# Five weight buffers and an earlier end of the weight splits, in a kernel of top-k attention and a gated FFN

## The chip, the cores and the metric

The kernel runs on one NeuronCore of a Trainium2 chip. The metric is device time in microseconds (us), lower is better. The engines are named as in the profile: PE (TensorE; PEld is its loading of weights), DVE (VectorE), ACT (ScalarE), POOL (GpSimd) and SP (SyncE, which here issues nearly all DMAs). Each engine works through its own list of instructions in order.

## The reference

Attention over 8 batches, 8 heads, 576 tokens and a head size of 64, in which every query keeps its 32 largest scores; then a gated feed-forward network (FFN) over all 4608 tokens. Everything is float32.

```python
scores = scale * np.matmul(q, k.transpose(0, 1, 3, 2))            # (8, 8, 576, 576)
kth = np.partition(scores, -top_k, axis=-1)[..., -top_k:-top_k + 1]
scores = np.where(scores >= kth, scores, -1000000000.0)
attn = np.exp(scores - np.max(scores, axis=-1, keepdims=True))
attn = attn / (np.sum(attn, axis=-1, keepdims=True) + 1e-09)
attn_out = np.matmul(attn, v)
x = attn_out.transpose(0, 2, 1, 3).reshape(4608, 512)
gate = 1.0 / (1.0 + np.exp(-(x @ w_gate)))                        # (4608, 1536)
return (gate * (x @ w_val)) @ w_out                               # (4608, 512)
```

## The kernel before

**Attention** goes in steps (loop variable `n`): a step is one block of 128 queries of a pair of heads in a batch. A step is named by batch, block and pair, as in e_0_3_2 (batch 0, block 3, pair 2). For a step PE makes the scores (pss; L269 and its neighbours in batch 0, L239 later), ACT copies them (s), DVE finds the 24 largest of 72-column segments (L338 to L344), ACT and POOL find what lies under them (L350, L356), DVE the threshold (L366), ACT the exponentials (L287), DVE the product with the mask (e, L292). PE transposes e (pt, L378), ACT copies that (et, L379), and PE multiplies by the values (po, L414), which gives the FFN's input xh and xl, an upper part and a rest.

**The FFN** works on units of tokens: units 0 to 2 have 256, the others 384. Its float32 products are made of three matmuls on upper parts and rests, so each weight tile is split too. There are 18 weight tiles of 1 MB: 0 to 11 hold gate and value weights (four to a group, three groups), 12 to 17 the output weights (two to a group). For a unit, `wide` does one tile of the first kind: 24 matmuls into pz (L475 to L477), the gate on ACT, DVE and ACT (gf, gh), the rest gl on POOL. `narrow` does half a tile of the second kind: 12 matmuls into po2 (L496 to L498; the profile writes po), added to acc.

**Splitting a weight tile** (`split_weights`) takes: a load of the raw tile (wraw, L135, a pool of two), ACT's L152 and L151, DVE's L153 (wt_lead, a pool of one), L161 and L162 (wt_frac, a pool of one), ACT's L163 (upper part), PE's L168, L169 and L170 (the rest, in PSUM), ACT's L171 (the rounded rest), and a store to DRAM (ws, L172). The result lies in a buffer of the pool "w". Tiles 4 to 11 and 14 to 17 are used from there by unit 0 (`fresh`; the profile writes w_split); all later uses load the tile again from DRAM into a buffer of the same pool (L461, tile w). The tiles are split in the order 0 to 3, 12, 13, 4 to 7, 14, 15, 8 to 11, 16, 17.

**What sets the order.** The loop over steps writes out attention, the splits that are due, and FFN tasks. `HELD`, 20, is the number of half splits (two to a tile) due by step `SOON`; the last 16, eight tiles, are spread evenly over the steps from there to `RUSH`:

```python
due = HELD * (n + 1) // SOON
if n >= SOON:
    due = HELD if not todo else HELD + (2 * n_w - HELD) * (n - SOON) // (RUSH - SOON)
```

`todo` is empty until unit 0's input is written out at the end of step 9, so these 16 half splits fall to the steps 10 and on. Unit 0's FFN tasks are written out between the splits, each as soon as its tile is split. When the last split is done the pools of the split are given back, and the pools that take their room open: among them one more score tile ("spare"), with which scores are made three steps ahead instead of two. What the loop writes out is then put into each engine's order by a scheduler that weighs priorities and readiness, at build time. A tile that needs a buffer waits until the last use of the tile five (or four) before it in its pool.

Of the kernel before, what the change touches and what calls it, by code (L numbers as in the profile page):

```python
# [30 lines left out]
def tile_topk_attention_then_gated_ffn(  # L31
# [19 lines left out]
    FG = NE = NP  # L51
# [15 lines left out]
    FETCH, ASK, AHEAD = 2, 4, 2  # L67

    orders = ([*range(1, NG), 0], [*range(NG)])
    SOON, RUSH = 8, 15  # L70
    RAISE = 200
    HELD = 2 * (2 * FG + NE // 2)
    MILES = [(512, 256), (832, 512), (1152, 768), (1536, 1152), (1984, 1536), (2624, 2112)]
# [35 lines left out]
    pools, fresh, copies, ahead, requests = {"first": bkr}, {}, [], [], []  # L109

    def ffn_pools():
        for name, bufs in (("w", 4), ("f2", 3), ("f4", NE), ("fg", FG + 1)):
            pools[name] = ctx.enter_context(tc.tile_pool(name=name, bufs=bufs))

    def split_weights():
# [401 lines left out]
    def run(general):  # L517
# [27 lines left out]
        if not general:  # L545
            ffn_pools()
            splits = split_weights()
# [176 lines left out]
```

## Time and profile before

| | us |
|---|---|
| median of 3 runs | 1564.49 |
| lowest and highest of them | 1562.36, 1564.89 |
| the profiled execution | 1562.55 |
| its span, from first to last instruction | 1560.7 |

Of the span PE is busy 97%, DVE 82%, ACT 72%, POOL 68%. A busy time is the union of an engine's instructions, so what is missing from the span is idle time. Matmuls overlap: the length of one is longer than the distance to the next (0.28 us against 0.12 for 256 columns).

### The profile page before, as it was taken

How to read it: one execution, taken by the hardware profiler on the slowest of the kernel's cores; microseconds unless marked ns; L12 is line 12 of the kernel's file. 1: busy time of each engine (PE TensorE's matmuls, PEld its weight loads, DVE VectorE, ACT ScalarE, POOL GpSimd, SP SyncE). 2: the span in 40 equal slices, each digit the busy share in tenths (PEclk: the TensorE clock that was granted, in tenths of full speed). 3: DMA queues.
4: the chain of work that ended last, by engine and by line, in shares of the span. 5: the costliest groups of instructions: out<-in, count | busy, mean ns of one | idle time of the engine just before them, and what ended most of it. 6: DMA issues, size and time to landing. Idle time of an engine off the chain costs nothing.

```text
span 1560.7 us, 33841 instructions
## 1 busy us (share of the span) xinstructions
PE 1510.3 (97%) x10586; PEld 1378.4 (88%) x10586; DVE 1284.5 (82%) x5806; ACT 1116.0 (72%) x2405; POOL 1063.5 (68%) x1756
## 2 busy tenths in 40 slices
PE   6779999999999999999999999999999999999998
PEld 2346689999999999899999999999999999999998
DVE  7999868999988789888988879988898888888311
ACT  8998968787877687776776766777777777677221
POOL 4666658898766786787666876787766886676211
PEclk8999999999999999999999999999999999999999
DMA  7763598887655755566555665565564675465574
GB/s 251 258 222 134 214 359 314 290 282 291 230 187 200 245 197 206 182 229 221 204 178 198 223 239 189 195 238 196 208 223 168 208 250 194 173 223 177 193 273 158
DMA packets 88894, 344.14 MB, mean 220 GB/s; under 512 B 9856, under 2 KB 36992, under 8 KB 57984
## 3 DMA queue, kind: packets, MB, share of 16 engines
q1 hardware_dynamic: 88560, 341.58, 62.5%
q8 instruction: 86, 1.41, 0.4%
q14 instruction: 104, 0.85, 0.2%
q10 hardware_dynamic: 144, 0.29, 0.1%
HBM read 313.52 MB, written 28.31 MB: 219 GB/s over the span
## 4 chain that ended last, share of the span: by engine, by line
PE 74%; DVE 9%; POOL 6%; ACT 6%; issue 2%; DMA 2%; SPq 0%; POOLq 0%; ACTq 0%
PE pz L476 11%; PE pz L477 11%; PE pz L475 11%; PE pss L239 8%; PE po L414 6%; PE pt L378 6%; PE po L496 5%; PE po L498 5%; PE po L497 5%; POOL u L356 3%; DVE cand L338 2%; DVE e L292 2%; PE po L428 2%; ACT e L287 2%; ACT under L350 1%
## 5 line engine op out<-in xcount | busy, mean ns | idle before, releaser
L356 POOL TENSOR_TENSOR u<-s,under 128x288 f32<-128x288 f32 x576 | 456.0, 814 | 138.1 <-ACT under L350 127.4
L338 DVE MAX8 cand<-s 128x8 f32<-128x72 f32 x2304 | 346.6, 217 | 64.6 <-ACT s L246 56.3
L475 PE MATMUL pz<-xh,w 128*128 128x384 f32 (+1 forms) x1184 | 390.4, 332 | 1.1 <-DVE acc L502 0.7
L477 PE MATMUL pz<-xh,w 128*128 128x384 f32 (+1 forms) x1184 | 391.1, 331 | 0.0
L476 PE MATMUL pz<-xl,w 128*128 128x384 f32 (+1 forms) x1184 | 390.1, 330 | 0.3 <-POOL xl L448 0.3
L292 DVE SCALAR_TENSOR_TENSOR e<-s,kths,e 128x576 f32<-128x576 f32 x288 | 280.7, 977 | 0.9 <-ACT e L287 0.7
L350 ACT ACTIVATE under<-s,leads 128x576 bf16<-128x576 f32 x288 | 222.6, 774 | 80.4 <-DVE leads L342 33.1
L366 DVE MAX8 kths<-u 128x8 f32<-128x584 f32 x288 | 219.1, 761 | 45.0 <-POOL u L357 43.3
L287 ACT ACTIVATE e<-s,st 128x576 f32<-128x576 f32 x288 | 209.6, 771 | 62.9 <-POOL st L346 62.4
L483 POOL TENSOR_TENSOR gl<-gf,gh 128x384 fp32r<-128x384 f32 (+1 forms) x156 | 151.6, 972 | 116.5 <-ACT gh L482 112.7
L475 PEld LDWEIGHTS pz<-xh,w 128*128 128x128 f32 x1184 | 222.8, 189 | 2.4 <-DVE acc L502 1.0
L476 PEld LDWEIGHTS pz<-xl,w 128*128 128x128 f32 x1184 | 223.3, 189 | 0.8 <-POOL xl L448 0.6
L477 PEld LDWEIGHTS pz<-xh,w 128*128 128x128 f32 x1184 | 223.1, 189 | 0.3
L379 ACT ACTIVATE et<-pt 128x384 f32<-128x384 f32 x384 | 177.9, 486 | 27.9 <-PE pt L378 26.0
L496 PE MATMUL po<-gh,w 128*128 128x384 f32 (+1 forms) x592 | 194.6, 334 | 0.7 <-DVE acc L502 0.6
L497 PE MATMUL po<-gl,w 128*128 128x384 f32 (+1 forms) x592 | 194.9, 330 | 0.0
L498 PE MATMUL po<-gh,w 128*128 128x384 f32 (+1 forms) x592 | 194.3, 330 | 0.0
L246 ACT ACTIVATE s<-pss 128x576 f32<-128x576 f32 x252 | 161.2, 640 | 41.3 <-PE pss L239 40.5
L378 PE MATMUL pt<-ident,e 128*128 128x128 f32 x1152 | 179.6, 274 | 7.9 <-ACT et L379 4.2
L239 PE MATMUL pss<-k,qh 128*128 128x288 f32 (+2 forms) x588 | 164.9, 298 | 1.5 <-ACT s L246 1.5
L378 PEld LDWEIGHTS pt<-ident,e 128*128 128x128 f32 x1152 | 140.9, 141 | 24.6 <-ACT et L379 6.4
L239 PE MATMUL pss<-k,ql 128*128 128x288 f32 (+2 forms) x588 | 159.9, 294 | 0.0
(108 smaller groups left out, 2897.3 us busy)
## 6 DMA issues: line engine op xcount, KB each, us to landing
w<-ws SPq DMA_DIRECT2D x222, 1024.0 KB, 5.0
v<-in_v_dram SPq DMA_DIRECT2D x68, 352.0 KB, 3.2
wraw<-in_w_dram SPq DMA_DIRECT2D x36, 512.0 KB, 4.9
ws<-w_split SPq DMA_DIRECT2D x18, 1024.0 KB, 4.6
qraw<-in_q_dram SPq DMA_DIRECT2D x140, 128.0 KB, 3.1
kraw<-in_k_dram SPq DMA_DIRECT2D x56, 288.0 KB, 4.0
out_dram<-acc SPq DMA_DIRECT2D x40, 192.0 KB, 4.8
out_dram<-acc SPq DMA_DIRECT2D x12, 128.0 KB, 5.3
```

Source lines behind the costliest of these rows:

```text
L239: nc.tensor.matmul(ps[:, half, o : o + n], x[:, h * P : (h + 1) * P], ks[h][:, k0 : k0 + n], start=t == 0, stop=t == len(todo) - 1,)
L287: nc.scalar.activation(e[:, j], s[:, j], AF.Exp, bias=st[:, j : j + 1], scale=1.0 / SHRINK)
L292: nc.vector.scalar_tensor_tensor(e[:, j], s[:, j], kth[j], e[:, j], op0=ALU.is_ge, op1=ALU.mult, accum_out=st[:, 4 + j : 5 + j])
L338: nc.vector.max(cand[:, j, 8 * g : 8 * g + 8], s[:, j, g * SEG : (g + 1) * SEG])
L356: nc.gpsimd.tensor_tensor(u[:, j, part], s[:, j, part], under[:, j, part], op=ALU.mult)
L378: nc.tensor.transpose(pt[:, c], ef[:, k0 : k0 + P], ident)
L475: nc.tensor.matmul(ps, wt[:, u, 0, d], xh, start=d == 0, stop=False)
L476: nc.tensor.matmul(ps, wt[:, u, 0, d], xl, start=False, stop=False)
L477: nc.tensor.matmul(ps, wt[:, u, 1, d], xh, start=False, stop=d == NP - 1)
L496: nc.tensor.matmul(ps, wt[:, e % 2, 0, f], gh, start=f == 0, stop=False)
L497: nc.tensor.matmul(ps, wt[:, e % 2, 0, f], gl, start=False, stop=False)
L498: nc.tensor.matmul(ps, wt[:, e % 2, 1, f], gh, start=False, stop=f == FG - 1)
```

## The change

Two numbers: the pool "w" has five buffers of 1 MB instead of four, and `RUSH` is 12 instead of 15. So the due number of half splits is 28, 32 and 36 (all) at steps 10, 11 and 12; before it was 24, 26, 29, 31, 33 and 36 at steps 10 to 15.

```diff
-    SOON, RUSH = 8, 15
+    SOON, RUSH = 8, 12
...
-        for name, bufs in (("w", 4), ("f2", 3), ("f4", NE), ("fg", FG + 1)):
+        for name, bufs in (("w", 5), ("f2", 3), ("f4", NE), ("fg", FG + 1)):
```

As built, all engines' orders differ from step (0, 2, 0) on. Three places follow.

DVE, before, from the split of tile 11 to that of tile 16 (names: kths, e are attention's of the steps (0, 4, 1) and on; gf_0_2_2 is unit 0, group 2, tile 10):

```order
L153 SCALAR_TENSOR_TENSOR wt_lead_11_1984<-wt_lead_11_1984,minus_zero_168 128x1024
L342 MAX leads_122<-cand_0_4_3_2861 128x8
L366 MAX kths_121<-u_0_4_1_2683 128x8
L161 TENSOR_SCALAR wraw_11_1981<-wt_lead_11_1984 128x1024
L292 SCALAR_TENSOR_TENSOR e_0_4_1_2682,st_0_4_1_2680<-s_0_4_1_2163,kths_121,e_0_4_1_2682 128x576
L162 SCALAR_TENSOR_TENSOR wt_frac_11_1985<-wraw_11_1981 128x1024
L366 MAX kths_121<-u_0_4_2_2770 128x8
L296 RECIPROCAL st_0_4_1_2680<-st_0_4_1_2680 128x1
L481 SCALAR_TENSOR_TENSOR gf_0_2_2_1975<-gf_0_2_2_1975,pz_0_2_2_1_1962 128x256
L366 MAX kths_121<-u_0_4_3_2866 128x8
L153 SCALAR_TENSOR_TENSOR wt_lead_16_2135<-wt_lead_16_2135,minus_zero_168 128x1024
L161 TENSOR_SCALAR wraw_16_2132<-wt_lead_16_2135 128x1024
```

DVE, the changed kernel, from the split of tile 11 to wt_frac of tile 17:

```order
L153 SCALAR_TENSOR_TENSOR wt_lead_11_1808<-wt_lead_11_1808,minus_zero_168 128x1024
L161 TENSOR_SCALAR wraw_11_1805<-wt_lead_11_1808 128x1024
L481 SCALAR_TENSOR_TENSOR gf_0_2_2_1799<-gf_0_2_2_1799,pz_0_2_2_1_1786 128x256
L162 SCALAR_TENSOR_TENSOR wt_frac_11_1809<-wraw_11_1805 128x1024
L153 SCALAR_TENSOR_TENSOR wt_lead_16_1960<-wt_lead_16_1960,minus_zero_168 128x1024
L161 TENSOR_SCALAR wraw_16_1957<-wt_lead_16_1960 128x1024
L162 SCALAR_TENSOR_TENSOR wt_frac_16_1961<-wraw_16_1957 128x1024
L481 SCALAR_TENSOR_TENSOR gf_0_2_3_1951<-gf_0_2_3_1951,pz_0_2_3_1_1938 128x256
L153 SCALAR_TENSOR_TENSOR wt_lead_17_2011<-wt_lead_17_2011,minus_zero_168 128x1024
L161 TENSOR_SCALAR wraw_17_2008<-wt_lead_17_2011 128x1024
L502 SCALAR_TENSOR_TENSOR acc_0_1_0_1473<-po2_0_2_0_1979,acc_0_1_0_1473 128x256
L162 SCALAR_TENSOR_TENSOR wt_frac_17_2012<-wraw_17_2008 128x1024
```

Attention's instructions, which stood between the splits, are gone from there: the four splits follow each other with only unit 0's FFN between.

ACT, before, from the split of tile 10 to that of tile 11 (under and et are attention):

```order
L151 ACTIVATE wt_lead_11_1984<-wraw_11_1981 128x1024
L171 ACTIVATE w_split_10_1844<-wrest_10_0_1936 128x512
L171 ACTIVATE w_split_10_1844<-wrest_10_1_1941 128x512
L379 ACTIVATE et_0_2_3_2629<-pt_0_3_3_0_2710 128x3x128
L379 ACTIVATE et_0_2_3_2629<-pt_0_3_3_1_2715 128x3x128
L350 ACTIVATE under_0_4_2_2771,sums_0_4_2_2768<-s_0_4_2_2579,leads_122 128x576
L163 ACTIVATE w_split_11_1980<-wt_lead_11_1984 128x2x512
L152 ACTIVATE minus_zero_168<-wraw_16_2132 128x1024
L480 ACTIVATE gf_0_2_2_1975<-pz_0_2_2_0_1949 128x256
L350 ACTIVATE under_0_4_3_2867,sums_0_4_3_2864<-s_0_4_3_2587,leads_122 128x576
L379 ACTIVATE et_0_2_3_2629<-pt_0_3_3_2_2720 128x3x128
L384 ACTIVATE et_0_4_0_2797<-pt_0_4_0_0_2798 128x4x128
```

ACT, the changed kernel, from the split of tile 10 to that of tile 16:

```order
L171 ACTIVATE w_split_10_1748<-wrest_10_1_1765 128x512
L480 ACTIVATE gf_0_2_2_1799<-pz_0_2_2_0_1773 128x256
L163 ACTIVATE w_split_11_1804<-wt_lead_11_1808 128x2x512
L152 ACTIVATE minus_zero_168<-wraw_16_1957 128x1024
L482 ACTIVATE gh_0_2_2_1771<-gf_0_2_2_1799 128x256
L151 ACTIVATE wt_lead_16_1960<-wraw_16_1957 128x1024
L171 ACTIVATE w_split_11_1804<-wrest_11_0_1816 128x512
L171 ACTIVATE w_split_11_1804<-wrest_11_1_1821 128x512
L163 ACTIVATE w_split_16_1956<-wt_lead_16_1960 128x2x512
L480 ACTIVATE gf_0_2_3_1951<-pz_0_2_3_0_1925 128x256
L152 ACTIVATE minus_zero_168<-wraw_17_2008 128x1024
L482 ACTIVATE gh_0_2_3_1923<-gf_0_2_3_1951 128x256
```

Here too attention is gone from between. L151 of tile 16 stands ahead of both L171 of tile 11, as it stood ahead of the second of them before.

SP, which issues the DMAs, before, from the store of tile 10 on (w_0_0 to w_0_3 are unit 0's loads of tiles 0 to 3):

```order
L172 DMA ws10_133<-w_split_10_1844 128x2048
L135 DMA wraw_17_2262<-in_w_dram 128x1024 x2
L172 DMA ws11_134<-w_split_11_1980 128x2048
L172 DMA ws16_139<-w_split_16_2131 128x2048
L461 DMA w_0_0_2312<-ws0_123 128x2048
L461 DMA w_0_1_2347<-ws1_124 128x2048
L461 DMA w_0_2_2382<-ws2_125 128x2048
L192 DMA kraw_5_0_0_5444<-in_k_dram 128x576
L192 DMA kraw_5_0_1_5450<-in_k_dram 128x576
L172 DMA ws17_140<-w_split_17_2261 128x2048
L211 DMA qraw_1_0_1_2659<-in_q_dram 128x256
```

SP, the changed kernel, from the store of tile 10 on:

```order
L172 DMA ws10_133<-w_split_10_1748 128x2048
L135 DMA wraw_17_2008<-in_w_dram 128x1024 x2
L172 DMA ws11_134<-w_split_11_1804 128x2048
L172 DMA ws16_139<-w_split_16_1956 128x2048
L461 DMA w_0_0_2058<-ws0_123 128x2048
L461 DMA w_0_1_2093<-ws1_124 128x2048
L461 DMA w_0_2_2128<-ws2_125 128x2048
L461 DMA w_0_3_2163<-ws3_126 128x2048
L192 DMA kraw_5_0_0_5444<-in_k_dram 128x576
L192 DMA kraw_5_0_1_5450<-in_k_dram 128x576
L172 DMA ws17_140<-w_split_17_2007 128x2048
L211 DMA qraw_1_0_1_2659<-in_q_dram 128x256
```

Four loads of w, not three, now stand ahead of the keys (kraw), of the store of tile 17 and of two loads of queries; the load of values ahead of the store of tile 10 is gone from there.

## Rows read from the trace of the kernel before

**Rows 1.** Page, busy us (share of the span) and instructions of two engines.
```profile
PE 1510.3 (97%) x10586; PEld 1378.4 (88%) x10586; DVE 1284.5 (82%) x5806; ACT 1116.0 (72%) x2405; POOL 1063.5 (68%) x1756
```

**Rows 2.** Busy time of each engine by stretch (columns in the first row).
```profile
core 0: us, PE busy (x) PEld busy (x) DVE busy (x) ACT busy (x) POOL busy (x), PEclk, DMA share, GB/s
...
98.00:112.00 14.00, 11.08 (x56) 7.97 (x58) 14.00 (x55) 12.32 (x22) 8.43 (x12) 0.88 0.71 273
112.00:143.00 31.00, 29.55 (x193) 21.07 (x188) 31.00 (x144) 25.88 (x56) 22.84 (x37) 1.00 0.30 100
143.00:176.00 33.00, 30.74 (x200) 21.18 (x199) 30.68 (x120) 31.43 (x61) 19.86 (x30) 1.00 0.60 207
176.00:207.00 31.00, 27.80 (x175) 21.75 (x171) 23.20 (x62) 23.26 (x42) 14.15 (x25) 1.00 0.66 241
207.00:278.00 71.00, 69.52 (x607) 63.69 (x607) 56.76 (x292) 53.39 (x129) 55.21 (x93) 1.00 0.92 347
278.00:1556.00 1278.00, 1273.22 (x9086) 1209.46 (x9084) 1040.38 (x4780) 881.63 (x1953) 888.26 (x1478) 1.00 0.62 214
```

**Rows 3.** PE's waits from 176 to 207: total us, times, longest us.
```profile
PE pz L477 <- ACT w_split L171: 1.6, 1, 1.6
PE po L498 <- ACT w_split L171: 0.8, 2, 0.6
PE wrest L170 <- DVE wt_frac L162: 0.8, 1, 0.8
```

**Rows 4.** PE's waits from 143 to 176, the same columns.
```profile
PE pt L378 <- ACT et L379: 1.4, 2, 0.7
PE pss L269 <- ACT s L270: 0.7, 1, 0.7
```

**Rows 5.** PE's waits over the whole span, first and last of 17 rows.
```profile
PE pss L269 <- ACT s L270: 11.6, 8, 3.7
...
PE po L424 <- DVE rs L440: 0.2, 1, 0.2
```

**Rows 6.** PE in order of time, 180 to 198: start us, us, instruction, idle before.
```profile
180.47 0.62 PE L170 MATMUL wrest<-wt_frac,plus 128*128 128x512 f32 x2
...
183.61 0.39 PE L477 MATMUL pz<-xh,w_split 128*128 128x256 f32 x1 [1.62 <-ACT w_split L171]
...
194.31 1.88 PE L168 MATMUL wrest<-wt_lead,ident 128*128 128x512 f32 x4
...
197.96 0.38 PE L498 MATMUL po<-gh,w_split 128*128 128x256 f32 x1 [0.60 <-ACT w_split L171]
```

**Rows 7.** ACT in order of time, 181 to 198.
```profile
181.96 1.11 ACT L151 ACTIVATE wt_lead<-wraw 128x1024 f32<-128x1024 f32 x1
182.97 1.07 ACT L171 ACTIVATE w_split<-wrest 128x512 fp32r<-128x512 f32 x2
...
194.44 1.37 ACT L152 ACTIVATE minus_zero<-wraw 128x1024 f16<-128x1024 f32 x1
...
196.29 1.14 ACT L151 ACTIVATE wt_lead<-wraw 128x1024 f32<-128x1024 f32 x1 [0.22 <-PE wrest L168]
197.33 1.06 ACT L171 ACTIVATE w_split<-wrest 128x512 fp32r<-128x512 f32 x2
```

**Rows 8.** Page, the mask products: count, busy us, mean ns, idle before.
```profile
L292 DVE SCALAR_TENSOR_TENSOR e<-s,kths,e 128x576 f32<-128x576 f32 x288 | 280.7, 977 | 0.9 <-ACT e L287 0.7
```

**Rows 9.** Tile wraw, 140 to 210: from issue to landing.
```profile
DMA to landing us min/median/max: 3.8/4.6/6.6
```

**Rows 10.** Page, DMA issues: loads of w, count, KB each, median us to landing.
```profile
w<-ws SPq DMA_DIRECT2D x222, 1024.0 KB, 5.0
```

**Rows 11.** Tile w, 190 to 240: from issue to landing.
```profile
DMA to landing us min/median/max: 6.0/8.9/11.0
```

**Rows 12.** SP's waits over the span, first row: total us, times, longest us.
```profile
SPq L461 <- PE pz L477: 282.6, 97, 7.2
```

**Rows 13.** SP in order of time, 189 us.
```profile
189.09 0.81 SPq L135 DMA_DIRECT2D wraw<-in_w_dram x2
```

## Prediction

> **What bounds the kernel now.** I read the busy times first. TensorE (PE) is busy 1510.3 us of the span, VectorE (DVE) 1284.5 [rows 1]: PE is the engine whose idle time can be won. Then I read the same table stage by stage, to see where PE idles [rows 2]. From 278 us to the end it idles 1278.00 - 1273.22 = 4.8 us in 1278. The idle time sits at the start: 2.9 us in 98 to 112, 1.5 in 112 to 143, 2.3 in 143 to 176, 3.2 in 176 to 207, 1.5 in 207 to 278. Until 143 us DVE has no idle time at all (31.00 of 31), so DVE sets the pace there; from 143 to 176 DVE (30.68 of 33) and ScalarE (ACT, 31.43 of 33) set it together. After that PE sets it.
>
> The list of what PE waited for says which waits these are. In 176 to 207 all three are for weight splits, 1.6 + 0.8 + 0.8 us: ACT's rounding of the rest (L171) and DVE's wt_frac [rows 3]. In 143 to 176 they are attention's: 1.4 for et, 0.7 for scores [rows 4]. In the list for the whole span, 17 rows that begin and end as shown, there is no row in which PE waits for a load of w [rows 5].
>
> **The change, part by part.**
>
> *The fifth buffer.* SP waits 282.6 us for PE to be done with a weight tile [rows 12]: a load goes out as soon as a buffer is free, so with four buffers each load has three tiles of PE's work to land in. 222 loads in some 1350 us are one tile in 6.1 us, so 18 us; landing takes 5.0 in the median [rows 10], and 6.0 to 11.0 in the busiest stretch, 190 to 240 [rows 11]. The fourth tile of cover isn't needed; after the splits I cost the buffer at nothing. If that cover were gone, PE would show waits for w, each worth what the landing exceeds the cover. Around 200 us four loads instead of three now stand ahead of the keys and the store of tile 17 in SP's order. The last of them waits for tile 16, as the third did before, so nothing behind it waits for a later event; one more MB goes ahead of the keys, which are first needed some 25 us on.
>
> *The earlier splits.* As built, the order parts from the old one at about 113 us, for the splits only from tile 15 on (143 us). Counted with durations of the trace, an estimate: DVE work ahead of wt_frac of tiles 15, 8 and 9 grows by 2 to 3 us, ahead of tile 10's it falls by 2.7, ahead of tiles 11, 16 and 17 by 8 to 10. What moved behind the splits is attention: between wt_frac of tiles 9 and 17, six mask multiplications (L292) of 0.98 us are gone [rows 8], 5.9 us, with maxima and smaller ones. It is not lost: DVE idles 7.8 us in 176 to 207 and 14.2 in 207 to 278 [rows 2], and can do it there. So DVE's and ACT's total work stays; what counts is which PE waits go.
>
> Tile 10: PE's last L170 was done at 180.47 + 0.62 = 181.09, but the matmuls went on only at 183.61, after a wait of 1.62 [rows 6], because L171 began only at 182.97, behind attention's operations and L151 of tile 11 on ACT [rows 7]. Now no attention stands between. In its place the first L170 must wait for wt_frac: by the same counting DVE is done with it at about 175.5 and PE asks for it at about 175.2, which is too near to call. I price this as the shorter waits of this kind, 0.6 us. Gain 1.0.
>
> Tiles 11, 16, 17: PE then runs through four splits and their 24 matmuls with nothing else to do, so each tile's own chain shows: L168 ends, ACT does L151 of the *next* tile, then L171, then PE's third matmul. Before the change this chain already ran so for tile 16: L168 from 194.31, L151 at 196.29 released by it, L171 at 197.33, PE back at 197.96 after 0.60 us [rows 6, 7]. I take 0.60 for 11 and 16 and 0.2 for 17, which has no next tile; together 1.4 against 0.8 + 0.8 now [rows 3]. Gain 0.2. Bounds: nothing (if PE's own L169 and L170 cover it) and 1.62 each, the longest wait of this kind, which would be +3.3 over the three.
>
> Raw tiles: the pool holds two, so the load of tile 16 waits for wt_frac of tile 10, that of 17 for 11. Before, that load of tile 17 went out at 189.09 [rows 13] and the first operation on it (L152) started at 194.44 [rows 7], 5.35 us later; one transfer takes 3.8 to 6.6 [rows 9]. In the new order ACT comes to tile 16 about 5.7 us after that event (L170, L168 and 24 matmuls on PE, then L480 and L163 on ACT). I put 0.3 us for both tiles; bounds 0 and 2 x 1.0.
>
> The waits of 143 to 176: two stand between the same neighbours as before; the third (0.7, for et) has new neighbours. Gain 0.4, bounds 0 and 0.7. In 207 to 278 idle is 1.5 us [rows 2]; the loads of unit 0's last group go out some 8 us earlier, and the first scores of batch 1 stand 8 us of PE work later. I take half, 0.7; bounds 0 and 1.5, and a loss as large.
>
> Sum: 1.0 + 0.2 + 0.4 + 0.7 - 0.3 = 2.0 us gained. The profiled execution took 1562.55 us (span 1560.7 and 1.85 around it), so it would take 1560.5; the median of the three runs shown is 1.9 above it, 1564.49, and the same step from there gives 1562.5.
>
> Two rules of the Trainium skill speak to this. What the row shows: where splits stood among attention, PE lost 1.62 us to L171 queued behind attention [rows 6, 7]; where they stood alone, 0.60. "Perfetto Trace Analysis", Optimization Strategy, says that stages with different limits may gain from being interleaved; the change does the opposite with the last four tiles. By the rule these would cost more, which is the third rival below; by the rows 0.6 a tile. The second: granted clock is 0.88 of full in 98 to 112, where PE idles 2.9 of 14 us, and 1.00 in 176 to 207, where it idles 3.2 of 31 [rows 2]. "TensorE: Matmul & The Clock Gate", on oscillation, says that idle stretches throttle the engine again. With waits of 0.6 us between 5 us of work I expect 1.00; one fall like that in 98 to 112 would cost 0.12 x 14 = 1.7 us.
>
> **The rivals.** *More is won.* If the earlier splits free PE from all that it waits for between 143 and 278 us, it gains 2.3 + 3.2 + 1.5 = 7.0: 1557.5. For it: DVE has 8 to 10 us less to do before the last splits. Against: the chain within a tile remains, and by the same counting PE's own work until the last of them falls by 4 to 5 us, so PE can't be there much earlier either.
>
> *Nothing changes.* The splits of 15, 8 and 9 come later by 2 to 3 us of DVE work, PE waits there, and what tiles 10 to 17 win is only given back: 1564.5. For it: until 176 us DVE has hardly any idle time to take the delay up [rows 2]. Against: the list of PE's waits for 143 to 176 has no row of a split [rows 4], so these tiles were early enough.
>
> *Slower: the last four tiles become one serial chain* (what the rule on interleaving would come to here). The place is L152 on the raw tiles 16 and 17. Cover is about 5.7 us; weight loads in 190 to 240 needed up to 11.0 [rows 11]. At that landing time each of the two tiles costs 5 us with nothing else on PE's list: 9 to 10 us less the gain, 1572. It decides from about 8.2 us landing on (2 x 2.5 us more than cover pays for the 2.0 gained and 3.1 beyond). Against: in 176 to 207 the DMA engines are busy 0.66 [rows 2], and raw transfers landed within 6.6.
>
> Besides, everything behind 207 us is in a new order, and its 4.8 us of idle after 278 are drawn anew: 3 us either way.
>
> **How the numbers follow.** 0.2% is 3.1 us, about what a measurement of this kernel tells from no change. Chances: the forecast 0.50 (-0.5 to -4, mostly inside 0.2%), more is won 0.22, nothing 0.14, the serial chain or a bad draw later 0.14. Faster: 0.22 and some 0.11 of the forecast, 0.33; slower 0.15 (the chain and a little of "nothing" with a bad draw); the same 0.52. Predicted: 1562.5. The range goes from the whole gain, 1557.5, to 1567.5, which takes in a chain that is half covered and the later draw; the full chain is left out.
>
> **What would show it.** Right: in 143 to 207 PE's idle falls from 5.5 to about 4; L171 waits of about 0.6 for tiles 11 and 16, one wait for wt_frac at tile 10; no row of PE for w; DVE idle in 180 to 200 and busy in 200 to 222; granted clock 1.00 from 112 us on. Wrong: idle of ACT before L152 for raw tiles, waits of PE for w around 205 to 220, a clock under 1.00 there, or a sum of idle after 278 that differs by more than 3 us.

## The result, and the profile after

The changed kernel takes 1575.38 us in the median of six runs (1574.82 to 1575.67), the kernel before 1564.69 beside it (six runs, 1562.36 to 1566.32): a ratio of 1.0069, 95% interval 1.0056 to 1.0082. It is slower by 10.7 us, well outside the range. The profiled execution took 1575.31 us, its span 1573.5 against 1560.7.

Busy time by stretch in the changed kernel, the columns of [rows 2]:

```profile
core 0: us, PE busy (x) PEld busy (x) DVE busy (x) ACT busy (x) POOL busy (x), PEclk, DMA share, GB/s
98.00:112.00 14.00, 10.00 (x48) 7.03 (x48) 12.48 (x51) 11.90 (x23) 6.51 (x10) 0.88 0.74 265
112.00:143.00 31.00, 29.06 (x201) 21.29 (x200) 30.89 (x146) 26.13 (x55) 25.23 (x38) 1.00 0.32 112
143.00:176.00 33.00, 31.87 (x206) 22.66 (x206) 32.86 (x120) 31.53 (x60) 16.30 (x23) 1.00 0.56 205
176.00:207.00 31.00, 28.50 (x179) 22.50 (x178) 19.38 (x52) 20.68 (x34) 8.72 (x19) 1.00 0.83 311
207.00:278.00 71.00, 69.50 (x618) 65.58 (x617) 59.95 (x285) 54.35 (x136) 57.41 (x102) 1.00 0.92 349
278.00:1556.00 1278.00, 1264.78 (x9001) 1198.73 (x9000) 1035.67 (x4792) 880.00 (x1956) 893.85 (x1482) 1.00 0.61 212
```

In 143 to 207 us, where the splits were moved, PE's idle time fell from 5.5 to 1.13 + 2.50 = 3.6 us. What was won there is small beside what came after it: from 278 us on PE idles 13.2 us in 1278 instead of 4.8.

What PE waited for from 176 to 207, to be read beside [rows 3]:

```profile
PE pz L477 <- ACT w_split L171: 1.1, 1, 1.1
PE po L498 <- ACT w_split L171: 1.0, 2, 0.8
PE wrest L170 <- DVE wt_frac L162: 0.4, 1, 0.4
```

And three rows of ACT's timeline, where it comes to the raw tiles of the last splits:

```profile
182.19 1.39 ACT L152 ACTIVATE minus_zero<-wraw 128x1024 f16<-128x1024 f32 x1 [0.54 <-DMA wraw<-in_w_dram]
188.41 1.36 ACT L152 ACTIVATE minus_zero<-wraw 128x1024 f16<-128x1024 f32 x1 [0.95 <-DMA wraw<-in_w_dram]
...
190.26 1.13 ACT L151 ACTIVATE wt_lead<-wraw 128x1024 f32<-128x1024 f32 x1 [0.23 <-PE wrest L168]
```

The serial chain that the prediction named as the slower rival shows in its beginnings: ACT waits 0.54 and 0.95 us for raw tiles. Only the first can reach PE, within the wait of 1.1 us for L171 above; behind the second, L151 waited for PE anyway (0.23 us, for L168). In the list of PE's waits over the whole span, now 20 rows, none is for a load of w.

**A ledger of lost time.** Windows cut the two kernels at different places of the work, so most numbers below are from a ledger: for each pair of neighbouring matmuls of a trace the time from start to start, less the usual one for that line and shape in the kernel before (its median; for the lines of attention whose median holds waits, the mean of the lowest 85%), summed up to a given time, less the same sum of the kernel before. It counts waits, half clock and mere wider spacing alike. At the end it must give the difference of the spans, and does: 12.7 against 12.8 us. One caution: the profiled execution of the kernel before took 1562.55 us, some 2 us less than the medians of its other runs, so totals stand about 2 us too high against the medians (the first experiment's own profiled execution was 3 us below its median, too); the steps between columns are what to read. A pair that lies across an edge goes whole to one side: at 98 us, and in the third and fourth experiments at 540, that moves a column by up to 1.5 us. In stretches where a kernel has the same order as the kernel before, the steps in these columns stay within 0.6 us.

| kernel | at 98 us | 278 | 310 | 420 | 540 | end | 98 to 278 | 310 to 420 | 540 to end |
|---|---|---|---|---|---|---|---|---|---|
| changed | +0.5 | -2.7 | -2.0 | +3.2 | +3.7 | +12.7 | -3.2 | +5.2 | +9.0 |

So three steps: the split stage wins 3.2 us, 310 to 420 us loses 5.2, and the long rest loses 9.0 in small waits.

### The profile page after: what moved, and what is told of

The parts are those of the page before. It is cut to its first block, busy times and chain, and to the rows that moved or that the text cites. A ratio compares the mean times of both kernels' runs of the same rounds, so it can differ in the third digit from the quotient of the medians.

```text
span 1573.5 us, 33811 instructions
## 1 busy us (share of the span) xinstructions
PE 1517.4 (96%) x10586; PEld 1384.8 (88%) x10586; DVE 1281.7 (81%) x5806; ACT 1112.8 (71%) x2405; POOL 1064.8 (68%) x1756
## 4 chain that ended last, share of the span: by engine, by line
PE 38%; DVE 6%; POOL 4%; ACT 3%; issue 1%; DMA 0%; POOLq 0%; ACTq 0%
PE pz L476 6%; PE pz L477 6%; PE pz L475 6%; PE pss L239 4%; PE po L496 3%; PE po L497 3%; PE po L498 3%; PE pt L378 3%; PE po L414 3%; POOL u L356 2%; DVE cand L338 2%; DVE kths L366 1%; DVE e L292 1%; ACT e L287 1%; PE po L428 1%
## 5 line engine op out<-in xcount | busy, mean ns | idle before, releaser
L356 POOL TENSOR_TENSOR u<-s,under 128x288 f32<-128x288 f32 x576 | 461.0, 822 | 125.8 <-ACT under L350 116.6
L338 DVE MAX8 cand<-s 128x8 f32<-128x72 f32 x2304 | 347.9, 218 | 81.9 <-ACT s L246 73.1
L292 DVE SCALAR_TENSOR_TENSOR e<-s,kths,e 128x576 f32<-128x576 f32 x288 | 279.2, 972 | 0.3
L378 PE MATMUL pt<-ident,e 128*128 128x128 f32 x1152 | 182.5, 277 | 8.8 <-DVE e L292 5.3
L246 ACT ACTIVATE s<-pss 128x576 f32<-128x576 f32 x252 | 161.3, 640 | 39.5 <-PE pss L239 39.1
L378 PEld LDWEIGHTS pt<-ident,e 128*128 128x128 f32 x1152 | 141.7, 142 | 26.7 <-DVE e L292 7.7
```

The source lines that it names most:

```text
L292: nc.vector.scalar_tensor_tensor(e[:, j], s[:, j], kth[j], e[:, j], op0=ALU.is_ge, op1=ALU.mult, accum_out=st[:, 4 + j : 5 + j])
L338: nc.vector.max(cand[:, j, 8 * g : 8 * g + 8], s[:, j, g * SEG : (g + 1) * SEG])
L356: nc.gpsimd.tensor_tensor(u[:, j, part], s[:, j, part], under[:, j, part], op=ALU.mult)
L378: nc.tensor.transpose(pt[:, c], ef[:, k0 : k0 + P], ident)
```

## The experiments

Theories at the start: **redraw** (the change alters the order which the scheduler draws for everything behind it, and that order, not a part of the change, carries the loss), **fifth buffer** and **earlier look-ahead** (each costs time by itself; look-ahead, because the "spare" pool opens three steps earlier). All differences are against the kernel before unless said otherwise. Beside the runs I compared the rows that TensorE executes in each kernel's built order, without the running numbers of tiles; "parts" and "joins" below are places in these lists, in us of the kernel before.

**1. The fifth buffer alone.** Kernel before with

```diff
-        for name, bufs in (("w", 4), ("f2", 3), ("f4", NE), ("fg", FG + 1)):
+        for name, bufs in (("w", 5), ("f2", 3), ("f4", NE), ("fg", FG + 1)):
```

> The weight pool has five buffers; the split stays beside seven steps, so nothing but the fifth buffer is changed. Theory 'fifth buffer' (loads of w tiles come one tile earlier, and the order behind the split stage is worse with them, whatever the split does): 1572 us or more, with some 10 us of idle TensorE after 278 us. Theory 'look-ahead' (the pools that the split stage leaves behind open three steps earlier, and with them scores, queries and keys are asked one step further ahead from the twelfth step on): 1563 to 1566 us, idle after 278 us about 5 us as before. Theory 'redraw' (each change of the order draws the small late waits anew, and no single part carries the loss): between 1562 and 1578 us, with late waits at other places than in the changed kernel.

1585.92 us, ratio 1.0129 (1.0113 to 1.0146): worse than both parts together.

**2. The earlier split alone.** Kernel before with

```diff
-    SOON, RUSH = 8, 15
+    SOON, RUSH = 8, 12
```

> Four weight buffers as before; the last eight tiles are split beside four steps. Theory 'fifth buffer': 1562 to 1565 us, the idle time of 143 to 207 us falls by some 2 us, idle after 278 us about 5 us. Theory 'look-ahead': 1572 us or more, with 10 us or more idle after 278 us. Theory 'redraw': between 1560 and 1578 us, with late waits at other places than in the changed kernel.

1575.78 us, ratio 1.0074 (1.0060 to 1.0088).

**3. The look-ahead begun where it was.** Changed kernel with

```diff
-                    next(splits, None)
-                    splits = None
+                    opening, splits = splits, None
...
+            if n == 15 and not general:
+                next(opening, None)
```

> The changed kernel (five buffers, split beside four steps), but the pools that follow the split stage open at the sixteenth step, as in the kernel before, and so the look-ahead of one more step begins there too. Theory 'look-ahead': 1562 to 1566 us, idle after 278 us about 5 us. Theory 'fifth buffer': 1572 us or more, as the changed kernel. Theory 'redraw': between 1560 and 1578 us, its late waits not those of the changed kernel.

1579.80 us, ratio 1.0096 (1.0080 to 1.0111).

**4. The phase of the extra score tile.** Changed kernel with

```diff
-    pools, fresh, copies, ahead, requests = {"first": bkr}, {}, [], [], []
+    pools, fresh, copies, ahead, requests = {"first": bkr}, {}, [], [None] * 2, []
```

> The changed kernel, with the count of scores tiles that decides which of them (every fifth) stands in the extra pool begun at two, so that the same steps use the extra pool as in the kernel before. Theory 'fifth buffer': 1572 us or more. Theory 'look-ahead' in the form that only the phase of every fifth tile matters: 1562 to 1566 us; in the form that the earlier look-ahead matters: 1572 us or more. Theory 'redraw': between 1560 and 1578 us.

1580.66 us, ratio 1.0101 (1.0086 to 1.0117).

Every single part is as slow as the whole or slower, and undoing the look-ahead doesn't help: "fifth buffer" can't explain the second experiment, "look-ahead" neither the first nor the third. But three of the four times lie above the range that I gave for "redraw", and against what I expected of it the late waits stood at the same places in all five kernels. The row lists say why: on TensorE the four experiments part from the changed kernel by 167 us and join its order, row for row, at 548 to 558 us. I call that common order tail A, and that of the kernel before tail B. So the question became which kernels have tail A, and whether one without the change can have it. Small moves of the FFN's pacing numbers (`MILES`, pairs of a token count and the goal for the FFN's work there) and of the priority of the matmuls that weigh the values (`RAISE`), neither of which is part of the change, draw such kernels.

**5. The changed kernel with tail B.** Changed kernel with

```diff
-    MILES = [(512, 256), (832, 512), (1152, 768), (1536, 1152), (1984, 1536), (2624, 2112)]
+    MILES = [(512, 248), (832, 512), (1152, 768), (1536, 1152), (1984, 1536), (2624, 2112)]
```

> The changed kernel with one number of the FFN's pacing moved (the first goal, 256 at 512 tokens, is 248). Its order on TensorE is, row for row, the changed kernel's up to about 167 us, that of the kernel before from about 285 to 785 us, and the changed kernel's again nearly everywhere after that. Read from the start of every sixth wide task, the changed kernel is 2 us ahead of the kernel before at 278 us, 2 to 3 us behind at 785 us and 12 us behind at the end. Theory 'redraw, by stretches' (the time of a stretch goes with the order drawn there): 2 us ahead until 785 us, then a loss of 10 us, 1571 to 1574 us in all, with the waits of 1010 to 1023 and 1369 to 1383 us as in the changed kernel and none of those of 396 to 404 us. Theory 'fifth buffer or earlier look-ahead as such' (they cost time in every order): 1575 us, and a loss in 285 to 785 us too.

1565.29 us, ratio 1.0005 (0.9996 to 1.0014): both parts of the change are in it, and the loss in total is gone. In the ledger at the end of this section its tail costs 0.6 us in place of 9.0; 5.0 are still lost between 310 and 420 us, against 3.4 won in the split stage.

**6. The kernel before with tail A.** Kernel before with

```diff
-    MILES = [(512, 256), (832, 512), (1152, 768), (1536, 1152), (1984, 1536), (2624, 2112)]
+    MILES = [(512, 256), (832, 520), (1152, 768), (1536, 1152), (1984, 1536), (2624, 2112)]
```

> The kernel before (four buffers, split beside seven steps) with one number of the FFN's pacing moved (512 at 832 tokens is 520). Its order on TensorE is that of the kernel before up to about 167 us, the changed kernel's, row for row, from about 310 to 785 us, and a third one after that. Theory 'redraw, by stretches': level with the kernel before at 278 us, 3 to 5 us behind at 785 us, and 1568 to 1578 us at the end. Theory 'fifth buffer or earlier look-ahead as such': neither is in it, so 1563 to 1566 us.

1574.88 us, ratio 1.0068 (1.0055 to 1.0082): neither part of the change is in it, and the loss is there (8.7 of it in the tail).

**7. The changed kernel with another priority.**

```diff
-    RAISE = 200
+    RAISE = 250
```

> The changed kernel with the priority of the matmuls that weigh the values (RAISE) 250 for 200. Its order is the changed kernel's to about 190 us, one of its own to 785 us, and after that, in 21 of 47 pieces of 200 rows, row for row that of the kernel before. Theory 'redraw, by stretches': 2 us ahead at 278 us, a loss drawn anew to 785 us (0 to 7 us by the draws so far), little loss after it: 1562 to 1570 us. Theory 'fifth buffer or earlier look-ahead as such': 1573 us or more.

1572.44 us, ratio 1.0048 (1.0034 to 1.0062).

**8. The kernel before with another priority.**

```diff
-    RAISE = 200
+    RAISE = 190
```

> The kernel before with RAISE 190 for 200. Its order is that of the kernel before, row for row, up to about 380 us, another one to 785 us, and close to that of the kernel before after that. Theory 'redraw, by stretches': level with it at 380 us, 0 to 8 us behind at 785 us, little more after it: 1565 to 1573 us. Theory 'fifth buffer or earlier look-ahead as such': 1563 to 1566 us.

1562.97 us, ratio 0.9988 (0.9979 to 0.9997).

The places that the expectations of 5 to 8 give were read wrongly. A row list holds the loop twice, the second time for the branch at the program's end, which isn't executed; I had spread both over the span. Put right: 5 leaves the changed kernel's order at 259 us and has tail B from 475 us to the end; 6 leaves that of the kernel before at 275 and has tail A from 549; 7 leaves the changed kernel's at 302 and 8 that of the kernel before at 730, both for good. So the figure of 1571 to 1574 for the fifth came from a tail that it doesn't have; "redraw", applied to the right places, says level, as measured. That of the seventh rested on the same error, and the eighth came out below the range of "redraw" (1565 to 1573), as its order changes less than I thought. Matched row by row in the traces, the places up to 310 us agree within 7 us and those behind come 6 to 28 us earlier (tail A from 533 to 544, the eighth's leaving at 703); no conclusion hangs on that.

What PE waited for from 549 to 1556 us, three kernels. The changed one:

```profile
PE pss L239 <- ACT s L246: 3.4, 3, 1.7
PE pt L378 <- DVE e L292: 2.8, 4, 1.2
PE po L414 <- ACT et L379: 1.0, 1, 1.0
PE po L496 <- DVE acc L502: 0.8, 2, 0.6
PE pz L476 <- POOL xl L448: 0.7, 1, 0.7
PE pt L378 <- DVE leads L342: 0.5, 1, 0.5
PE pt L378 <- ACT et L384: 0.5, 1, 0.5
```

The sixth experiment, the kernel before drawn into tail A:

```profile
PE pt L378 <- DVE e L292: 2.9, 4, 1.3
PE pss L239 <- ACT s L246: 2.9, 3, 1.8
PE pt L378 <- DVE leads L342: 1.1, 1, 1.1
PE po L414 <- ACT et L379: 1.0, 1, 1.0
PE po L496 <- DVE acc L502: 0.9, 2, 0.6
PE pz L476 <- POOL xl L448: 0.7, 1, 0.7
```

The fifth, the changed kernel drawn into tail B:

```profile
PE pz L475 <- DVE acc L502: 0.7, 1, 0.7
PE pt L378 <- ACT et L379: 0.7, 1, 0.7
PE po L496 <- DVE acc L502: 0.6, 1, 0.6
PE po L414 <- ACT et L379: 0.5, 1, 0.5
PE pt L378 <- DVE e L292: 0.4, 1, 0.4
PE pz L476 <- POOL xl L448: 0.4, 1, 0.4
PE pss L239 <- ACT s L246: 0.2, 1, 0.2
```

The first two lists have nearly the same waits, in number and in the longest; the third has those of the kernel before (0.7, 0.7, 0.6, 0.5, 0.3, 0.2, 0.2). Waits of 9.7 and 9.5 us against 3.5 go with the order, whatever the two numbers of the change are.

One of these waits followed back in the changed kernel, rows of DVE, POOL, ACT and PE in order of time:

```profile
1017.61 0.90 DVE L292 SCALAR_TENSOR_TENSOR e<-s,kths,e 128x576 f32<-128x576 f32 x1
1018.43 0.23 DVE L338 MAX8 cand<-s 128x8 f32<-128x72 f32 x1
1018.73 2.07 POOL L196 TENSOR_TENSOR k<-kraw,k 64x288 fp32r<-64x288 f32 x2
...
1019.23 0.91 DVE L292 SCALAR_TENSOR_TENSOR e<-s,kths,e 128x576 f32<-128x576 f32 x1
...
1020.08 0.34 DVE L342 MAX8 tops<-cand 128x8 f32<-128x64 f32 x2
1020.89 0.22 POOL L346 TENSOR_SCALAR st<-tops 128x2 f32<-128x2 f32 x1
...
1021.14 1.45 ACT L287 ACTIVATE e<-s,st 128x576 f32<-128x576 f32 x2 [2.78 <-POOL st L346]
...
1024.49 0.63 ACT L246 ACTIVATE s<-pss 128x576 f32<-128x576 f32 x1
...
1025.17 0.40 PE L239 MATMUL pss<-k,qh 128*128 128x288 f32 x1 [1.74 <-ACT s L246]
```

ACT waits 2.78 us for the small L346 on POOL, and its copy of scores (L246), queued behind, makes PE wait 1.74. L346 has two things before it that end nearly together. It reads the largest score of both heads. Counted from the start of the trace, DVE comes to the second head's last segment (L338) at 1018.43, behind a mask product (L292), and brings its maximum (L342) by 1020.42, behind another. A pair of key subtractions (L196), ahead of L346 on POOL, ends at 1020.80. So the pair accounts for half a us of ACT's wait at most, an estimate from these rows; most of it is the order on DVE. The sixth experiment has the same rows 2.2 us earlier, with 2.80 on ACT and 1.8 on PE. This wait is the largest; tail A has a dozen waits, most of them under 1.3 us.

**9 to 11. Tail B with each part, and the best of both.** The next three put single parts of the change onto tails known to be good: the second experiment with another goal, the first with another, and the ninth with RAISE 190 (all against the kernel before; the lines of 9, 10 and 11 in this order, the ends of the MILES lines left out).

```diff
-    SOON, RUSH = 8, 15
+    SOON, RUSH = 8, 12
-    MILES = [(512, 256), (832, 512), ...
+    MILES = [(512, 256), (832, 528), ...
```

```diff
-        for name, bufs in (("w", 4), ("f2", 3), ("f4", NE), ("fg", FG + 1)):
+        for name, bufs in (("w", 5), ("f2", 3), ("f4", NE), ("fg", FG + 1)):
-    MILES = [(512, 256), (832, 512), ...
+    MILES = [(512, 256), (832, 508), ...
```

```diff
-    SOON, RUSH = 8, 15
-    RAISE = 200
+    SOON, RUSH = 8, 12
+    RAISE = 190
-    MILES = [(512, 256), (832, 512), ...
+    MILES = [(512, 256), (832, 528), ...
```

> Four buffers, split beside four steps, as the second experiment, with one pacing goal moved (512 at 832 tokens is 528). On TensorE its order is the second experiment's to about 240 us, one of its own to 498 us, and from there, row for row, that of the kernel before. Theory 'redraw' (the order drawn between 240 and 500 us, and the tail that it falls into, make the loss; the split stage keeps what it has won): 3 to 4 us ahead at 237 us, as the second experiment; 2 to 5 us of that given back to 500 us; level from there on, no loss of 7 to 8 us in the tail: 1561 to 1566 us. Theory 'earlier split costs time in every order': 1572 us or more, as the second experiment. Sub-theory 'the fifth buffer costs the split stage 2 to 3 us': 1 to 2 us better than the fifth experiment (five buffers, same tail), so 1562 to 1564 us.

> Five buffers, split beside seven steps, as the first experiment, with one pacing goal moved (512 at 832 tokens is 508). Its order is the first experiment's to about 270 us, one of its own to 782 us, and from there, row for row, that of the kernel before. Theory 'redraw' with 'the fifth buffer costs the split stage 2 to 3 us': 3 us behind at 237 us, 1 to 8 us more to 782 us, nothing after it: 1568 to 1576 us, against 1586 us with the other tail. Theory 'redraw' with a free fifth buffer: level at 237 us, 1565 to 1573 us. Theory 'fifth buffer costs time in every order': 1580 us or more.

> The ninth experiment with RAISE 190 for 200. Its order is the ninth's to about 730 us and from there, row for row, that of the eighth experiment (the kernel before with RAISE 190), whose tail ended level with that of the kernel before by the profile and 2 us ahead by the medians. Theory 'redraw': what the ninth gives, less 0 to 2 us: 1559 to 1565 us, and the best of the kernels so far. Theory 'earlier split costs time in every order': 1570 us or more.

9: 1565.19 us, ratio 1.0000 (0.9992 to 1.0009). 10: 1570.18 us, 1.0034 (1.0022 to 1.0045), where the same buffer with tail A had 1585.92. 11: 1564.13 us, 0.9992 (0.9983 to 1.0001), within its range, but not the best so far, which is the eighth. The split stage keeps its gain in 9, and no late loss follows; yet the kernel isn't faster, as 3.4 us go between 310 and 420. And 9 is no better than 5 (1565.19 and 1565.29): that the fifth buffer costs 2 to 3 us in the split stage fell, with the split beside four steps. With the split beside seven steps it costs something (+2.4 and +2.7 from 98 to 278 in 1 and 10, after a loss of 4.6 and 4.9 before 143 us); why only there stays open.

**12 to 15. Redraws of the kernel before.** Every kernel with a part of the change loses 3.4 to 5.2 us between 310 and 420. Is that the order drawn there again, or does the earlier split itself provoke it? The kernel before, with one number moved in each:

```diff
-    RAISE = 200
+    RAISE = 250
```

```diff
-    MILES = [(512, 256), ...
+    MILES = [(512, 264), ...
```

```diff
-    MILES = [(512, 256), (832, 512), ...
+    MILES = [(512, 256), (832, 504), ...
```

```diff
-    MILES = [(512, 256), (832, 512), ...
+    MILES = [(512, 256), (832, 528), ...
```

> The kernel before with RAISE 250 for 200; on TensorE its order leaves that of the kernel before at 210 us and doesn't come back to it. Theory 'the order drawn decides': it loses 2 to 6 us from 310 to 420 us against the kernel before, as the kernels with the change do. Theory 'the earlier split makes the loss': it loses less than 2.5 us there. The tail is a new one: 0 to 12 us by the tails so far, 1565 to 1580 us in all.

> The kernel before with the pacing goal 264 for 256 at 512 tokens; its order leaves that of the kernel before at 241 us for good. Theory 'the order drawn decides': it loses 2 to 6 us from 310 to 420 us. Theory 'the earlier split makes the loss': less than 2.5 us there. A new tail: 1565 to 1580 us in all.

> The kernel before with the pacing goal 504 for 512 at 832 tokens; its order leaves that of the kernel before at 291 us for good. Theory 'the order drawn decides': it loses 2 to 6 us from 310 to 420 us. Theory 'the earlier split makes the loss': less than 2.5 us there. A new tail: 1565 to 1580 us in all.

> The kernel before with the pacing goal 528 for 512 at 832 tokens; its order leaves that of the kernel before at 275 us and has it again, row for row, from 382 us on. Theory 'the order drawn decides': it loses 1 to 4 us from 310 to 420 us, and nothing after it: 1564 to 1569 us. Theory 'the earlier split makes the loss': level with the kernel before at 420 us and at the end, 1563 to 1566 us.

12: 1584.27 us, ratio 1.0134 (1.0117 to 1.0151). 13: 1571.71, 1.0054 (1.0037 to 1.0071). 14: 1571.13, 1.0051 (1.0034 to 1.0067). 15: 1567.68, 1.0019 (1.0009 to 1.0030). All four are slower than the kernel that they differ from by one number. The 2 to 6 us that "the order drawn decides" gave for 310 to 420 came in 12 and 14 (2.7 and 3.5); 13 lost 1.8, which the other theory allowed too, and 15 lost 4.6, more than the 1 to 4 expected. The total of 12 lies above its range.

What PE waited for from 310 to 420 us in the fifteenth, whose order differs from that of the kernel before only between 275 and 382 us:

```profile
PE pss L239 <- ACT s L246: 1.1, 1, 1.1
PE pt L378 <- ACT et L379: 1.0, 2, 0.7
PE po L496 <- DVE acc L502: 0.8, 1, 0.8
```

The same stretch of the changed kernel:

```profile
PE rb L431 <- ACT et L384: 1.3, 1, 1.3
PE po L497 <- POOL gl L483: 1.0, 1, 1.0
PE po L496 <- DVE acc L502: 0.4, 1, 0.4
PE pss L239 <- ACT s L246: 0.2, 1, 0.2
PE po L496 <- DVE gf L481: 0.2, 1, 0.2
```

The kernel before has one wait there, 0.5 us for s. The whole ledger:

| kernel | 98 to 278 | 310 to 420 | 540 to end | end | tail |
|---|---|---|---|---|---|
| changed | -3.2 | +5.2 | +9.0 | +12.7 | A |
| 1 five buffers | +2.4 | +4.5 | +10.2 | +20.3 | A |
| 2 RUSH 12 | -4.0 | +4.3 | +9.1 | +12.2 | A |
| 3 look-ahead late | -0.6 | +4.8 | +8.9 | +15.1 | A |
| 4 phase | -2.9 | +5.1 | +10.6 | +17.6 | A |
| 5 changed, 248 | -3.4 | +5.0 | +0.6 | +2.3 | B |
| 6 before, 520 | -0.2 | +2.3 | +8.7 | +10.6 | A |
| 7 changed, RAISE 250 | -5.5 | +5.2 | +6.3 | +9.9 | own |
| 8 before, RAISE 190 | +0.5 | +0.2 | -0.3 | +0.2 | C |
| 9 RUSH 12, 528 | -3.2 | +3.4 | +0.4 | +2.8 | B |
| 10 five buffers, 508 | +2.7 | +5.1 | -2.3 | +7.5 | B from 782 |
| 11 as 9, RAISE 190 | -3.9 | +3.5 | -0.1 | +2.6 | C |
| 12 before, RAISE 250 | +0.8 | +2.7 | +16.7 | +21.2 | own |
| 13 before, 264 | +0.5 | +1.8 | +7.0 | +9.1 | own |
| 14 before, 504 | +0.4 | +3.5 | +3.2 | +8.5 | own |
| 15 before, 528 | +0.6 | +4.6 | +0.5 | +5.9 | B |

Down the column "540 to end" the tail decides: six kernels with A, one of them without the change, lose 8.7 to 10.6; B costs 0.4 to 0.6 in the three that have it from 540 us or earlier, with and without the change; the other four drawn orders cost 3.2 to 16.7. B and C are the two cheapest of the seven seen. Only the tenth was better in a long stretch: on its own order, before it joins B, it gains over 2 us on the kernel before (from 540 to 800 us PE idles nothing there, 1.4 us in the kernel before). Some of these numbers hold a fall of the clock worth 1.7 us (last section): 310 to 420 of the changed kernel and of 15, and the tails of 4, 7, 12 and 13.

## Why the prediction was wrong

**The step that failed** is the last sentence of the rivals: "everything behind 207 us is in a new order, and its 4.8 us of idle after 278 are drawn anew: 3 us either way." The mechanism was named, its size had no row, and it is not symmetric. Measured, the ledger goes from -2.7 at 278 us to +12.7 at the end, a loss of 15.4 us; 9.5 of it is idle time up to each kernel's last FFN matmul (13.3 against 3.8; the 4.8 hold 1.0 behind that matmul) and 1.7 a fall of the clock (last section); the rest is matmuls that start further apart without idle time that the profile shows. Idle time of 4.8 us in 1278 can fall by little and can rise by much. Of the fifteen experiments eleven are slower than the kernel before by more than their interval and one is faster; of the six orders of the tail other than B, five lose 3 to 17 us. I gave a "bad draw later" and the serial chain together 0.14. A term that spans 82% of the time was priced by feel, while a wait of 0.6 us was traced through four engines.

**What was right, and what was luck.** The split stage won about what was forecast: -3.2 us from 98 to 278 in the ledger against 2.0 forecast (-2.9 to -5.5 in the kernels with the split beside four steps, but for the third, -0.6). In PE's idle time, the prediction's own terms, it won 1.8 from 143 to 278 (5.1 against 6.9) and lost 1.6 from 98 to 143, so nearly nothing; the ledger's gain is for the most part matmuls that start nearer to each other without idle time that the profile shows, 2.1 us of it at the transposes (L378). No term of the prediction stood for that, so the agreement of the totals is in part luck. Term by term: tile 10's wait for L171 gave way to one for wt_frac of 0.4 (0.6 forecast); the L171 waits that remain are 1.1 + 1.0 = 2.1 us against 1.4 forecast, so the term of tiles 11, 16 and 17 was a loss of 0.5 (2.1 against 0.8 + 0.8), not a gain of 0.2, and up to 0.5 of it is the wait for a raw tile, priced apart at 0.3 (ACT came to the raw tiles some 5.0 and 4.4 us after the event that sends their loads off, not 5.7); the waits of 143 to 176 fell by 1.1 (one of 1.0 is left, [rows 4] had 2.1), not 0.4; 207 to 278 won nothing (1.50 against 1.48 idle), not 0.7. 98 to 143, which I left out as unchanged, idles 5.9 us instead of 4.4. DVE idled from 180 to 200 and was busy from 200 to 222 as forecast (busy 11.0 of 20 us, then 17.7 of 22; in the kernel before 16.8 and 8.6). Of the signs of being wrong two came: ACT's idle time before L152 and the idle time after 278.

**The fifth buffer** was rightly costed at nothing in this change: with RUSH 12 the pairs with five and four buffers (changed and 2; 5 and 9) lie within 0.8 us in the split stage, and no wait for w appears. Alone, with RUSH 15, it isn't free (1, 10).

**The rivals.** "More is won" and "nothing changes" didn't occur; the serial chain was there for 0.54 + 0.95 us of ACT's time, and its price of 9 to 10 us didn't come; that its 1572 lies nearer to the measured time than the forecast does is chance. The Trainium skill, "Perfetto Trace Analysis", Optimization Strategy, says that stages with different limits may gain from being interleaved; that the four splits set apart would therefore cost isn't borne out by the rows: L171 waits of 2.1 us stand against 2.4 in [rows 3]. The clock was 1.00 from 112 to 278 as forecast; it fell once later (below).

**What stays open.** The loss between 310 and 420: redrawn orders without the change (6, 12 to 15) lose 1.8 to 4.6 there, 3.0 in the mean; the ten kernels with a part of it lose 3.4 to 5.2, 4.6 in the mean. So a redraw alone makes most of it, shown by the fifteenth: without the fall of the clock it loses 2.9, the changed kernel 3.5. Whether the rest, 1.6 us between the means, is the earlier split's own (PE might arrive ahead of DVE, which isn't shown) or chance, ten and five draws don't settle, and the ten are not independent: 9 and 11 have the same rows there. Nor do the runs say why the scheduler falls into the same tail A from six starting points; that needs its inner state. And the gain of the split stage was never kept: no kernel with the change beats the kernel before by more than its interval. The only kernel that does is the eighth, without the change: the kernel before with RAISE 190, by 0.12% (0.03 to 0.21), less than the 0.2% named as the bound.

## What to carry to other kernels

Where a scheduler draws one order for a whole program, an edit of one stage is two changes: the stage, which a profile can price, and a redraw of all that follows, which it can't. Ask how good the present draw is: when the long rest idles 0.4% of its time, the new one will more likely be worse, and the forecast belongs on that side. To test an edit, run it with several neutral draws, and compare stretch by stretch, not only totals.

Build orders can be compared without a run: where two kernels have the same rows, expect the same waits. That crosses an edit with an order (experiments 5 and 6), which settles in two runs what undoing parts one by one couldn't.

## What was unexpected of the hardware

Repeatability: once the order is the same, waits of 0.5 to 1.8 us come back in another kernel at the same operation, mostly to 0.1 us, up to 800 us behind the place where the kernels last differed. Of the changed kernel's 13 waits behind 549 us ten stand before the same matmul in the sixth experiment within 0.13 us, two are there with another length, one is missing.

The clock. In the changed kernel the granted clock fell once in the middle of dense work. Busy time of PE, granted clock and DMA in three stretches, and below them the stretch of such a fall in the fifteenth experiment:

```profile
400.00:405.00 5.00, 3.09 (x22) 1.00 0.57 210
405.00:409.00 4.00, 4.00 (x38) 0.57 0.68 180
409.00:420.00 11.00, 11.00 (x76) 1.00 0.39 137
```

```profile
319.00:323.00 4.00, 4.00 (x22) 0.57 0.98 276
```

PE idled 1.9 of 5 us, in no wait longer than 1.3, and then the clock stood at its lower level, 1.2 GHz, for part of the next 4 us. Worked out from the row, they lost 0.43 x 4 = 1.7 us: a third of the changed kernel's loss between 310 and 420 us in the profiled execution. The seventh and twelfth experiments show the same at 664 us (in the seventh after a wait of 2.2 us), the thirteenth at 661, the fourth at 1029, after 2.8 us of idle in nine. The Trainium skill, "TensorE: Matmul & The Clock Gate", in its section on a second failure mode, tells of a kernel whose TensorE idles briefly and often between groups of matmuls, by which its clock goes back and forth; the short waits ahead of these falls agree.

But the same waits needn't bring it. All six kernels with tail A have waits of 0.95 to 0.98 and of 1.74 to 1.77 us, 7 us apart, before the same two matmuls near 1018 and 1025 us (in the changed kernel's time); only the fourth experiment's clock fell there. So small waits can cost more than themselves, and one profile of a kernel doesn't tell whether they always do.
